# Attention with chunk selection, then a gated MLP, on one core: K^T of two head pairs made on TensorE instead of by DMA, under a new instruction order

## The chip, the cores and the metric

The kernel runs on one core of one Trainium2 chip. The metric is the device time of one launch in microseconds. The core has TensorE (PE; its weight loads are PEld), VectorE (DVE), ScalarE (ACT), GpSimd (POOL) and SyncE (SP), which here issues all DMAs. Matmul results land in PSUM, everything else lies in SBUF.

## What is computed

q, k and v are 4 x 8 x 768 x 64 (batch, heads, positions, head width), in float32. Keys are taken in 24 chunks of 32. For every query an upper bound of its score with each chunk is taken from the chunk's minimum and maximum of k; the six best chunks are kept, the rest is masked, and a causal softmax attention runs over what is left. Its output goes through a gated block with a spatial mix.

```python
ub = sum(maximum(q * k_min, q * k_max))          # per query and chunk
top_chunks = argsort(where(causal, ub, -1e9))[..., -6:]
attn = softmax(where(selected & causal, q @ k.T / 8, -1e9))
x = attn @ v                                     # 4 x 768 x 512
h = gelu(x @ w_in); u, v = h[..., :512], h[..., 512:]
v_n = (v - mean(v)) / sqrt(var(v) + 1e-6) * g_ln
out = x + (u * (w_sg @ v_n + b_sg)) @ w_out
```

## The kernel before, in words

**Pairs and batches.** The 32 heads are worked on in 16 pairs p of two heads; pairs 4b to 4b + 3 make batch b. Position blocks are 128 long (six of them). For each pair the program has K^T and Q^T in bf16 (tiles KA and QA, four buffers, index p % 4), V with a column of ones (vx), the selection, six score pieces (PSUM tiles PSC, two buffers), exponentials into E (ScalarE, L784 and L833), a triangle set to zero on the diagonal blocks (POOL, L789 and L840), P V (TensorE, L856 and L863), and a division into XS (VectorE, L871 and L873; below "rcp" and "xs"). When the four pairs of a batch are done, x is transposed (TensorE L890 for batches 0 and 3, DMA L882 for 1 and 2; "dt_x") and the MLP runs: hv (L905, the half that is normalised), hu (L945), the mix pt (L962) with two VectorE steps (L968, L972), the output ou (L981), the residual sum os (L988) and the store (L992).

**Two ways to K^T.** For pairs below KD = 8, `kside` loads k in two DMAs, transposes it on TensorE in float32 (L524, "ktr"), takes each chunk's minimum and maximum from PSUM on VectorE (L563, "kmm"), and copies K^T out of PSUM to KA ("kev": four copies of 64 x 384 for pairs 4 and up). From pair KD on, `kside_full` loads k in one DMA, takes minimum and maximum with a transposing reduction (L580, "kred"), casts k to bf16 with mask columns beside it (tile kbx, or the tile of IND used again; "kcast"), and lets SP issue two DMA transposes into KA (L587, "kT"). The reductions of two pairs are then put in place by one group of small matmuls (L602, "perm") and two copies (L610, "wcp"). Both ways end in W, with a small subtraction ("wsub", L573 or L615).

**Selection.** From pair 4 on, two pairs are selected together (`select_full`): the bounds by small matmuls (L709, "ub"), a transpose (L718, "utr"), the eight largest (L729, "m8"), a comparison (L734, "dn"), a transpose back (L737, "dt"), and four small DMAs that write the mask rows into QA (L742, "qd"; qd_8_1 is pair 8, head 1). The scores of the pair ("sc", L778) wait for them.

**Order.** Nothing is scheduled at run time. The table TABLE holds, for each of the five engines, the numbers of its operations in the order in which they run, a PSUM slot for each tile, and, under "engine", the engine of those copies and casts that could run on more than one (`flex`, L435 to L438: a name such as kev_4_0_0 or qcast_3 with act or dve; without an entry the copy has its usual engine). `Program.place` takes order and slots, `Program.link` works out the semaphore waits. Engines that touch the same PSUM tile wait for each other in program order, also when both only read. On each engine, and in SP's queue, everything behind a waiting instruction waits too.

Of the kernel before, what the change touches and what calls it, by code (L numbers as in the profile page):

```python
# [261 lines left out]
def _build(nc, ctx, q, k, v, w_in, g_ln, w_sg, b_sg, w_out, out):  # L262
# [46 lines left out]
    NBULK = 0  # L309
    XROW = 940  # L310
    DXT = tuple((b, d) for b in (1, 2) for d in range(4))
    KD = 8
    WSGT = False
    GROUPS = [(0,), (1,), (2,), (3,)] + [(a, a + 1) for a in range(4, NP, 2)]
    NW = 4
# [430 lines left out]
    def mask_rows(w):  # L746

        for i in range(2):
            m0 = 64 * (1 - i)
            if w + HALF < KD:  # L750
                flex("pool", ("act",), lambda i=i, m0=m0: KA[w][i][m0:m0 + 64, :], lambda m0=m0: INDF[m0:m0 + 64, :], S,
# [268 lines left out]

    if KD < NP:
        kb_init(0)
# [24 lines left out]
    for p in range(4, NP + 4):  # L1047
# [19 lines left out]

TABLE = {
# [16 lines left out]
    "act": (  # L1085
# [10 lines left out]
    "dve": (  # L1096
# [16 lines left out]
    "pool": (  # L1113
# [13 lines left out]
    "slots": (  # L1127
        "10230231221303100111101110030212010101231013110010132121001110101032100101010103200010112322333223233223"
        "22322333232201110033100011112311100101100123001100012310011023233232232233323233333233220100102201111000"
        "23101010110101231010110032100101232332322223332332332323232210101023000110122000110123101011123020301213"  # L1130
        "33210130111302021102"),
    "filler": (
        "49:8 "),
    "engine": (
        "rel_0:act rel_1:act wic_0:act kcast_9_0:act rel_7:act rel_6:act woc_0:act kcast_8_0:act qcast_7_1:act "
        "qcast_6_0:act kcast_9_1:act rel_8:act kcast_8_1:act kcast_11_0:act qcast_10_0:act rel_11:act "
        "vhat_1_2:act vhat_1_0:act kcast_13_1:act qcast_12_0:act rel_14:act vcast_14:act vhat_3_3:act "
        "vhat_3_5:act vhat_3_0:act qev_0_1:dve kev_0_1:dve kev_2_1:dve qev_2_1:dve wev_1_1:dve qev_2_0:dve "
        "wev_1_0:dve qev_4_0:dve kev_4_1_0:dve kev_4_0_0:dve xev_0_0:dve wev_0_0:dve qev_5_1:dve kev_5_0_0:dve "
        "kev_5_0_1:dve kev_5_1_1:dve vhat_0_3:dve vhat_0_4:dve vhat_0_1:dve vhat_0_0:dve vhat_0_2:dve "  # L1140
        "qev_10_1:dve qev_13_0:dve xev_3_0:dve xev_3_2:dve "),
}


# [57 lines left out]
```

## Time and profile before

| | us |
|---|---|
| median of 3 runs | 223.46 |
| their lowest and highest | 222.56, 226.68 |
| the profiled execution | 224.85 |
| its span, first to last instruction | 223.1 |

In the views of the profile "busy" is the time in which an engine's instructions ran; "idle before" is the time in which it stood before an instruction, with what ended that wait; "x" counts instructions. L778 is line 778. A name out<-in tells the tile that is written and those that are read. SPq is SP's queue of DMA issues. The span is also cut into 40 equal slices of 5.6 us, and a digit tells the busy share of each in tenths.

### The profile page before, as it was taken

The numbers are of one execution on the slowest core, as the hardware profiler recorded it, in microseconds if no ns is written. First come the engines' busy times: TensorE is split into PE (matmuls) and PEld (weight loads), VectorE is DVE, ScalarE is ACT, GpSimd is POOL, SyncE is SP. The second block draws the span as 40 slices with busy tenths as digits, with TensorE's granted clock in tenths as the row PEclk, the third lists the DMA queues.
The fourth block names the chain that finished last, engine by engine and source line by source line (L and its number), as shares of the span: only waits on it lengthen the run. The fifth ranks groups of instructions, "written<-read, shape, count | busy, mean of one in ns | idle before, by whom it ended". The sixth has DMA issues, their size and how long they took to land.

```text
span 223.1 us, 6031 instructions
## 1 busy us (share of the span) xinstructions
PE 203.6 (91%) x2397; PEld 131.1 (59%) x2397; DVE 185.3 (83%) x526; ACT 165.3 (74%) x247; POOL 96.4 (43%) x135
## 2 busy tenths in 40 slices
PE   7689959989999999885999999999799999999993
PEld 3456738855765657664445676776544668655551
DVE  4999972979999999899599998875699776695993
ACT  3879857997899997895768986986966888667000
POOL 7626877595224367476113076745233124002000
PEclk9999996999999999999699999999999999999999
DMA  7999999979269999799999969938941103000306
GB/s 153 218 250 209 268 208 325 347 164 207 87 159 242 239 233 217 169 175 150 201 201 180 254 135 226 228 92 207 162 101 28 36 0 144 3 0 0 144 29 253
DMA packets 101403, 37.06 MB, mean 166 GB/s; under 512 B 95616, under 2 KB 96384, under 8 KB 101376
## 3 DMA queue, kind: packets, MB, share of 16 engines
q1 hardware_dynamic: 101376, 36.68, 76.7%
q8 instruction: 19, 0.31, 0.6%
q14 instruction: 8, 0.07, 0.1%
HBM read 24.77 MB, written 6.29 MB: 139 GB/s over the span
## 4 chain that ended last, share of the span: by engine, by line
PE 62%; DVE 20%; DMA 6%; ACT 5%; SPq 3%; issue 2%; POOL 1%; DVEq 0%
PE PSG L962 12%; PE PSG L905 9%; PE PSC L778 8%; PE PSG L981 6%; PE PSG L945 5%; PE PSG L524 5%; PE PSG L856 4%; DVE Wall L563 3%; PE PSC L818 3%; ACT E L784 2%; DMA out_dram<-osb 2%; PE PSG L709 2%; DMA kn<-in_k_dram 2%; DVE U L718 2%; DVE osb L988 2%
## 5 line engine op out<-in xcount | busy, mean ns | idle before, releaser
L784 ACT ACTIVATE E<-PSC 128x1024 bf16<-128x1024 f32 (+1 forms) x72 | 62.8, 919 | 13.4 <-PE PSC L778 10.8
L778 PE MATMUL PSC<-QA,KA 128*128 128x128 bf16 (+2 forms) x336 | 37.4, 247 | 3.6 <-DMA QA<-Dt 2.1
L789 POOL TENSOR_SCALAR_AFFINE_SELECT E<-E 128x768 bf16<-128x768 bf16 x24 | 21.0, 879 | 37.4 <-ACT E L784 37.4
L962 PE MATMUL PSG<-wsgT,vhat 128*128 128x384 bf16 x192 | 34.8, 326 | 0.5 <-DVE rden L871 0.5
L778 PEld LDWEIGHTS PSC<-QA,KA 128*128 128x128 bf16 x336 | 23.8, 98 | 14.4 <-ACT E L784 5.1
L438 POOL CAST QA<-qT 64x768 bf16<-64x768 f32 (+1 forms) x24 | 21.2, 885 | 13.9 <-DVE qT L438 4.9
L962 PEld LDWEIGHTS PSG<-wsgT,vhat 128*128 128x128 bf16 x192 | 18.0, 98 | 11.2 <-ACT uT L950 0.6
L905 PE MATMUL PSG<-winb,xT 128*128 128x512 bf16 x96 | 23.0, 384 | 1.8 <-issue 1.3
L945 PE MATMUL PSG<-xT,winb 128*128 128x384 bf16 x128 | 23.7, 327 | 0.0
L950 ACT ACTIVATE uT<-PSG 128x384 bf16<-128x384 f32 x32 | 15.2, 487 | 11.2 <-PE PSG L945 11.0
L981 PE MATMUL PSG<-woutb,uT 128*128 128x512 bf16 x96 | 23.4, 379 | 0.1
L968 DVE SCALAR_TENSOR_TENSOR PSG<-PSG,glnT,bsgbc 128x384 f32<-128x384 f32 x32 | 19.7, 618 | 4.1 <-PE PSG L962 3.5
L833 ACT ACTIVATE E<-PSC 128x1024 bf16<-128x1024 f32 (+1 forms) x24 | 20.7, 924 | 3.0 <-PE PSC L824 2.9
L856 PE MATMUL PSG<-vx,E 128*128 128x65 bf16 x480 | 20.2, 195 | 1.6 <-DVE XS L873 1.3
L988 DVE TENSOR_TENSOR osb<-PSG,XS 128x512 f32<-128x512 f32 x24 | 16.0, 684 | 6.4 <-PE PSG L981 4.7
L856 PEld LDWEIGHTS PSG<-vx,E 128*128 128x128 bf16 x480 | 17.9, 99 | 3.7 <-DVE XS L873 1.8
L909 ACT ACTIVATE vgb<-PSG 128x512 f32<-128x512 f32 x24 | 14.0, 597 | 7.5 <-PE PSG L905 7.4
L563 DVE TENSOR_REDUCE Wall<-PSG 128x12 f32<-128x384 f32 x32 | 16.0, 543 | 2.7 <-PE PSG L524 2.6
L873 DVE TENSOR_TENSOR XS<-PSG,rden 128x384 bf16<-128x384 f32 x32 | 17.6, 552 | 0.7
L972 DVE TENSOR_TENSOR uT<-PSG,uT 128x384 bf16<-128x384 f32 x32 | 17.4, 551 | 0.5
L945 PEld LDWEIGHTS PSG<-xT,winb 128*128 128x128 bf16 x128 | 11.5, 98 | 9.4 <-ACT uT L950 2.1
L524 PE MATMUL PSG<-identF,qn 128*128 128x128 f32 x96 | 15.1, 278 | 1.7 <-DMA qn<-in_q_dram 1.0
(107 smaller groups left out, 363.1 us busy)
## 6 DMA issues: line engine op xcount, KB each, us to landing
qn<-in_q_dram SPq DMA_DIRECT2D x32, 192.0 KB, 4.1
vn<-in_v_dram SPq DMA_DIRECT2D x16, 384.0 KB, 5.2
out_dram<-osb SPq DMA_DIRECT2D x24, 256.0 KB, 2.3
kn<-in_k_dram SPq DMA_DIRECT2D x16, 192.0 KB, 4.6
kn<-in_k_dram SPq DMA_DIRECT2D x8, 384.0 KB, 4.1
uT<-in_moe_w_sg_dram SPq DMA_DIRECT2D x4, 384.0 KB, 6.5
vgb<-in_moe_w_in_dram SPq DMA_DIRECT2D x3, 512.0 KB, 6.2
QA<-Dt SPq DMA_DIRECT2D x24, 36.0 KB, 2.7
```

The costliest lines, as they stand in the source:

```text
L438: return e.tensor_copy(dst(), src())
L524: r = e.matmul(t.ap()[:, 128 * j:128 * j + 128], src[:].rearrange("p i t d -> p (i t d)")[:, 128 * x:128 * x + 128], identF[:], is_transpo ...
L563: P.op("dve", lambda d, m=m, op=op, t=t, hf=hf: d.tensor_reduce(W[w][:, m, 12 * hf:12 * hf + 12], t.ap()[:, 0:TG].rearrange("p (c x) -> p ...
L778: r = e.matmul(t.ap()[:, o:o + n], KA[w][i][:, 128 * kb:128 * kb + 128], QA[w][i][:, q0:q0 + n], start=True, stop=True)
L784: P.op("act", lambda e, t=t, c0=c0, c1=c1, i=i: e.activation(E[es][:, i, c0:c1], t.ap()[:, 0:c1 - c0], ACTF.Exp, scale=SCALE), act(c1 - c0 ...
L789: P.op("pool", lambda g, ev=ev: g.affine_select(ev, ev, pattern=[[0, NT], [1, 128]], compare_op=ALU.is_ge, fill=0.0, base=0, channel_multi ...
L833: P.op("act", lambda e, t=t, c0=c0, c1=c1, n=n: e.activation(E[es][:, :, c0:c1], t.ap().rearrange("p (i x) -> p i x", i=2)[:, :, 0:n], ACT ...
L856: r = e.matmul(t.ap()[:, 65 * qb:65 * qb + 65], E[es][:, i, a:a + 128], vx[w][:, kb, i, :], start=first, stop=False, skip_group_check=True)
L905: r = e.matmul(t.ap()[:, 0:F], xT[s][:, dk, 128 * qt:128 * qt + 128], winb[:, dk, F:DFF], start=(dk == 0), stop=(dk == NDK - 1))
L945: r = e.matmul(t.ap()[:, 0:TG], winb[:, dk, 128 * fb:128 * fb + 128], xT[s][:, dk, TG * tg:TG * tg + TG], start=(dk == 0), stop=(dk == NDK ...
L962: r = e.matmul(t.ap()[:, 0:TG], vhat[s][:, sb, 128 * fb:128 * fb + 128], wsgT[:, sb, TG * tg:TG * tg + TG], start=(sb == 0), stop=(sb == N ...
L981: r = e.matmul(t.ap()[:, 0:DM], gT[s][:, fb, 128 * qt:128 * qt + 128], woutb[:, fb, :], start=(fb == 0), stop=(fb == NF - 1))
```

## The change

KD goes from 8 to 10, so pairs 8 and 9 get their K^T in the first of the two ways. This renumbers the operations, and the whole table is replaced: the order on every engine, the PSUM slots, and the list of engines. No operation is computed otherwise than before apart from pairs 8 and 9.

```diff
-    KD = 8
+    KD = 10
...
     "engine": (
-        "rel_0:act rel_1:act wic_0:act kcast_9_0:act rel_7:act rel_6:act woc_0:act kcast_8_0:act qcast_7_1:act "
-        "qcast_6_0:act kcast_9_1:act rel_8:act kcast_8_1:act kcast_11_0:act qcast_10_0:act rel_11:act "
-        "vhat_1_2:act vhat_1_0:act kcast_13_1:act qcast_12_0:act rel_14:act vcast_14:act vhat_3_3:act "
-        "vhat_3_5:act vhat_3_0:act qev_0_1:dve kev_0_1:dve kev_2_1:dve qev_2_1:dve wev_1_1:dve qev_2_0:dve "
-        "wev_1_0:dve qev_4_0:dve kev_4_1_0:dve kev_4_0_0:dve xev_0_0:dve wev_0_0:dve qev_5_1:dve kev_5_0_0:dve "
-        "kev_5_0_1:dve kev_5_1_1:dve vhat_0_3:dve vhat_0_4:dve vhat_0_1:dve vhat_0_0:dve vhat_0_2:dve "
-        "qev_10_1:dve qev_13_0:dve xev_3_0:dve xev_3_2:dve "),
+        "qcast_0:act mrow_0_1_0:act rel_1:act qcast_3:act wic_0:act rel_5:act mrow_3_0_0:act qcast_4_0:act "
+        "rel_6:act rel_7:act kcast_10_1:act woc_2:act woc_3:act rel_8:act rel_10:act rel_11:act qcast_11_0:act "
+        "rel_12:act vhat_1_0:act kcast_13_1:act rel_13:act kcast_13_0:act rel_14:act vhat_3_2:act vhat_3_5:act "
+        "kev_0_0:dve qev_0_0:dve kev_2_1:dve kev_2_0:dve qev_2_0:dve kev_3_1:dve kev_4_0_1:dve kev_4_0_0:dve "
+        "kev_4_1_0:dve kev_4_1_1:dve kev_5_0_1:dve xev_0_0:dve qev_5_1:dve kev_5_0_0:dve xev_0_1:dve xev_0_3:dve "
+        "kev_5_1_1:dve kev_5_1_0:dve kev_7_1_0:dve vhat_0_3:dve vhat_0_5:dve vhat_0_4:dve vhat_0_1:dve "
+        "vhat_0_0:dve qev_15_0:dve xev_3_0:dve xev_3_1:dve xev_3_2:dve xev_3_3:dve "),
```

The rest of the table are numbers. In names, and to the point of the prediction, the orders read as follows (before, then after; each engine by itself, excerpts).

```
PE    ub_8 sc_7_1_2 ... pv_7_1 pvd_7_1 pv_7_0 pvd_7_0 qtr_12_1 qtr_12_0 sc_8_1_0 sc_8_1_1 ub_10 sc_8_1_2 hv_1_1
PE    perm_10 ... ub_8 ... pv_7_0 pvd_7_0 pv_7_1 pvd_7_1 qtr_12_1 qtr_12_0 ub_10 sc_8_1_2 sc_8_1_0 hv_1_1

DVE   utr_8 m8_8_0 m8_8_1 rcp_6_1 dn_8 xs_6_1 rcp_6_0 dt_8 xs_6_0 rcp_7_1 xs_7_1 rcp_7_0 xs_7_0
DVE   utr_8 m8_8_1 rcp_6_0 m8_8_0 xs_6_0 rcp_6_1 xs_6_1 dn_8 dt_8 rcp_7_0 xs_7_0 rcp_7_1 xs_7_1

POOL  kcast_11_1 qcast_9_0 aff_6_0 aff_7_1 qcast_8_0 kcast_10_1 aff_7_0
POOL  aff_6_0 vcast_6 kcast_11_0 vcast_8 aff_7_0 aff_6_1 vcast_7 aff_7_1 qcast_10_1

SP    kT_8_1 qn_12_1 kT_8_0 kn_14 dt_x_1_1 dt_x_1_0 qd_8_1 dt_x_1_2 dt_x_1_3 qn_13_0 qd_8_0
SP    dt_x_1_0 qn_13_0 qn_12_1 vn_7 qn_11_1 dt_x_1_1 kn_12 dt_x_1_2 qd_8_1 dt_x_1_3 qn_13_1 qd_8_0

SP    qn_1_0 kn_2_0 kn_2_1 qn_2_1 qn_3_0 qn_2_0 qn_3_1 ws_1
SP    qn_1_1 ws_1 kn_2_1 kn_2_0 qn_3_1 qn_2_1 qn_2_0 qn_3_0
```

(kn, qn and vn load a pair's k, q and v; qtr transposes q on TensorE; aff is the triangle of E; ws loads a tile of w_sg; vcast and qcast cast v and q to bf16.)

More of the change, by code (lines that the diff above doesn't have):

```diff
@@ L1069 @@
     "pe": (
[15 rows of a table removed]
-    "act": (
[10 rows of a table removed]
-    "dve": (
[16 rows of a table removed]
-    "pool": (
[13 rows of a table removed]
[15 rows of a table added]
+    "act": (
[10 rows of a table added]
+    "dve": (
[17 rows of a table added]
+    "pool": (
[12 rows of a table added]
     "slots": (
[L1128 to L1131, printed above, removed]
+        "23102213010323200101101110130011110010232110001110123120310010010032011111010102300110103332323232322232"
+        "33223222332301100032000000111023111101011010320110011032101010232332332233222333333222323210011033100111"
+        "10321001010111012311101000320101012323323332232223322233232233001110231001101321110010320100101231213003"
+        "2032111012311302030302"),
     "filler": (
```

106 rows, old and new, of the table TABLE are left out of this document.

## The prediction

> **What bounds the kernel now.** I read the page first (busy shares, the 40 slices), then the busy time by stage, then the chain of waits and the timeline at the two places where TensorE stops, then the groups by line and shape for prices.
>
> ```profile
> span 223.1 us, 6031 instructions
> PE 203.6 (91%) x2397; PEld 131.1 (59%) x2397; DVE 185.3 (83%) x526; ACT 165.3 (74%) x247; POOL 96.4 (43%) x135
> PE   7689959989999999885999999999799999999993
> PEclk9999996999999999999699999999999999999999
> ```
>
> TensorE is busy 91% of the span: 19.5 us are left. Its digits fall at the start, in slices 6 and 19 (a 5 each) and in the last one, and the granted clock has a 6 in the slice behind each of the two 5s. The stretches below (columns: window and its length, then busy us of PE, PEld, DVE, ACT, POOL, clock, DMA share, GB/s) are my stages: up to the last transpose of x for batch 0, up to the selection of pairs 8 and 9, up to the MoE of batch 1, up to the MoE of batch 2, and the rest.
>
> ```profile
> 0.00:46.60 46.60, 39.36 (x605) 28.23 (x605) 36.49 (x120) 35.59 (x52) 31.14 (x52) 0.96 1.05 241
> 46.60:93.65 47.05, 45.02 (x490) 29.49 (x490) 44.48 (x128) 41.54 (x72) 23.04 (x33) 1.00 0.88 196
> 93.65:109.00 15.35, 11.73 (x204) 7.99 (x203) 12.32 (x39) 11.35 (x16) 8.93 (x12) 0.91 1.02 162
> 109.00:159.70 50.70, 48.53 (x621) 31.22 (x620) 43.35 (x134) 42.03 (x59) 21.41 (x27) 0.99 1.01 188
> 159.70:223.10 63.40, 58.98 (x482) 34.17 (x482) 48.61 (x108) 34.80 (x51) 11.93 (x13) 0.99 0.24 73
> ```
>
> The second stage is full on two engines (TensorE 45.0 and VectorE 44.5 of 47.05), so work added there counts in full. The fourth and fifth are TensorE's, with 2.2 us idle and, in the fifth, 3.7 us of stores behind the last matmul. Time can be won in the first and the third. What happens there:
>
> ```profile
> 31.45 0.54 DVE L438 CAST KA<-PSG 64x384 bf16<-64x384 f32 x1
> 32.02 0.48 ACT L435 ACTIVATE KA<-PSG 64x384 bf16<-64x384 f32 x1 [2.53 <-DVE KA L438]
> 32.52 1.30 ACT L833 ACTIVATE E<-PSC 128x1024 bf16<-128x1024 f32 x2
> 33.60 0.39 PE L818 MATMUL PSC<-QA,KA 64*128 64x384 bf16 x4 [2.64 <-ACT E L833]
> ```
>
> ScalarE stood 2.53 us before one copy of pair 4's K^T, because VectorE held the same PSUM tile for its half of it; the exponentials queue behind that copy on ScalarE, and the scores of pair 2 (TensorE, 2.64 us idle) wait for an exponential to free their PSUM. In the third stage:
>
> ```profile
> 98.08 1.99 DVE Dn L734
> 100.69 1.29 SPq L882
> 102.03 3.34 DMA QA<-Dt
> 105.42 1.05 PE PSC L778 x11
> 106.47 2.10 PE PSG L709 x32
> ```
>
> This is the chain of pair 8: compare (Dn), transpose, the small DMA that puts the mask rows into QA (it stood in SP's queue behind an x transpose), then the scores. Both stops are followed by a slow clock:
>
> ```profile
> 31.00:33.60 2.60, 0.00 (x1) 0.01 (x2) 1.37 (x4) 1.57 (x3) 2.37 (x4) 1.00 0.76 168
> 33.60:38.60 5.00, 5.00 (x73) 4.21 (x73) 1.43 (x5) 3.78 (x7) 4.00 (x5) 0.66 1.08 322
> 105.42:109.10 3.68, 3.68 (x47) 1.83 (x48) 1.03 (x2) 1.94 (x2) 0.00 (x0) 0.63 0.73 160
> 155.00:160.00 5.00, 3.73 (x82) 2.71 (x64) 3.26 (x16) 4.98 (x7) 0.05 (x1) 1.00 1.00 131
> ```
>
> At 0.66 for 5.00 us and 0.63 for 3.68 us the lost clock is 5.00 x 0.34 = 1.7 us and 3.68 x 0.37 = 1.4 us. The stop of 1.27 us before 159.7 (last row: 5.00 - 3.73) is followed by none.
>
> **The change, part by part.** *K^T of pairs 8 and 9.*
>
> ```profile
> L580 DVE TRANSPOSE_TENSOR_REDUCE Bn<-kn 128x24 f32<-128x768 f32 x16 | 15.2, 962 | 0.0
> L563 DVE TENSOR_REDUCE Wall<-PSG 128x12 f32<-128x384 f32 x32 | 16.0, 543 | 2.7 <-PE PSG L524 2.6
> L610 DVE COPY Wall<-PSG 128x48 f32<-128x48 f32 x8 | 1.4, 201 | 0.7 <-PE PSG L602 0.7
> L524 PE MATMUL PSG<-identF,kn 128*128 128x128 f32 x48 | 7.5, 282 | 1.6 <-DMA kn<-in_k_dram 1.0 <-ACT KA L435 0.6
> L602 PE MATMUL PSG<-Bn,identF 64*32 64x24 f32 x128 | 1.6, 191 | 0.0
> L435 ACT ACTIVATE KA<-PSG 64x384 bf16<-64x384 f32 x11 | 5.3, 481 | 2.7 <-DVE KA L438 2.5
> L435 ACT ACTIVATE kbx<-kn 128x384 bf16<-128x384 f32 x2 | 1.1, 542 | 0.0
> L587 SPq DMA_TRANSPOSE KA<-kbx x8: 1248/1290/2101, 93.8 to 159.9; - x8
> L742 SPq DMA_DIRECT2D QA<-Dt x24: 507/591/2139, 59.7 to 173.3; - x24
> ```
>
> TensorE: 12 transposes come, 12/48 x 7.5 = 1.9 us; one group of 32 small matmuls goes, 32/128 x 1.6 = 0.4: +1.5 us, in the full second stage: on the path. VectorE: 8 reductions come, 8/32 x 16.0 = 4.0; 4 long ones go, 4/16 x 15.2 = 3.8; two 201 ns copies go and one small subtraction comes: about even, 0. ScalarE: 8 copies come, 8 x 0.481 = 3.8; 4 casts go, 4 x 0.542 = 2.2: +1.7 us, beside TensorE (41.5 of 47.05 busy); if that cover were gone it would cost all of it. SP's queue: 4 transposes at 1.29 us go, and two whole loads of K are split into four. Nobody waits for these transposes (pair 8's scores wait for QA<-Dt), so I cost the freed queue at nothing; the ends are 0 and 4 x 1.29 = 5.2 us of earlier issues.
>
> *Other engines.* Over the whole kernel VectorE is handed 18 movable copies and gives 15; ScalarE takes five casts of 768 columns from POOL ahead of its first gelu (qcast_0, qcast_3, qcast_4_0, two mask rows) and gives two 768-column evictions of x; the rest goes one for one.
>
> ```profile
> L435 ACT ACTIVATE QA<-qT 64x768 bf16<-64x768 f32 x4 | 3.3, 836 | 0.0
> L435 ACT ACTIVATE xT<-PSG 128x768 bf16<-128x768 bf16 x5 | 4.0, 809 | 2.1 <-PE PSG L890 2.1
> L438 DVE CAST KA<-PSG 64x384 bf16<-64x384 f32 x5 | 2.7, 546 | 0.0
> ```
>
> ScalarE in the first stage: 35.6 + 5 x 0.84 - 2 x 0.81 = 38.2 us. VectorE there is handed ten and gives eight, 36.5 + 2 x 0.55 = 37.6 us.
>
> *First stage in the new order.* All four quarter-copies of pair 4's K^T now lie on VectorE, so ScalarE no longer stands before one of them, and the exponentials run on. The gain is at most the stop and its clock, 2.6 + 1.7 = 4.3 us. TensorE's work there is the same, 39.4 - 1.7 = 37.7 us at full clock, with VectorE 37.6 and ScalarE 38.2: three engines equally full trip over each other, and w_sg's second tile is now loaded ahead of pair 2's K. What is late next is VectorE's K^T and q copies of pairs 4 and 5. I take -2.5 us, nearer to the full price, since the copy that caused it is gone; ends -4.3 and +2.6 (ScalarE's extra work with its 11.0 us of idle time kept).
>
> *Second stage.* +1.5 us, as above; ends 0 (its 2.0 us of idle time take it) and +3.
>
> *Third stage.* The selection matmuls of pairs 10 and 11 (L709, the 2.10 us row, 1.2 us at full clock) now stand ahead of pair 8's scores instead of behind, and so fill the stop; xs_6 goes ahead of dn_8 on VectorE, so that pair 7's P V no longer waits for it:
>
> ```profile
> 100.60 0.64 PE L856 MATMUL PSG<-vx,E 128*128 128x65 bf16 x15 [0.91 <-DVE XS L873]
> 101.80 0.62 PE L856 MATMUL PSG<-vx,E 128*128 128x65 bf16 x15 [0.38 <-DVE XS L873]
> 105.42 1.05 PE L778 MATMUL PSC<-QA,KA 128*128 128x128 bf16 x11 [2.13 <-DMA QA<-Dt]
> ```
>
> But the chain grows by one xs (0.55 us), and qd_8_1 now stands behind three x transposes in SP's queue, of which the last is ready before dn_8. Idle is 0.91 + 0.38 + 2.13 = 3.4 us plus 1.4 of clock. Filling 1.2 of it is sure if the chain keeps its length; the shorter stop may spare the clock. I take -1.5; ends -4.8 (all of it) and +2.1 (rival 3).
>
> The page "TensorE: Matmul & The Clock Gate" of the Trainium skill, Part 1, says that the clock falls after an idle window of about 3.4 us that runs free. Here stops of 2.64 and 2.13 us were enough and 1.27 was not, so the measurement decides; if the page's figure were a threshold, no stop here would pay for a slow clock, and the sum would be about 1 us less of a gain.
>
> *Fourth and fifth stage.* Same instructions in nearly the same places on TensorE; the stop before batch 2's MoE waits for x transposes that hang on pair 11's heads, as before. 0; ends -1 and +3, since an order this dense can get a new wait of the size of the two above.
>
> **The sum.** -2.5 + 1.5 - 1.5 + 0 = -2.5 us. The profiled execution took 224.85 us (span 223.1 and 1.75 around it), so one like it would take 222.4; the median of the runs shown is 223.46, 1.4 below, so I forecast 221.0.
>
> **The rivals.** (1) *Both stops go in full*, the second with its clock (2.13 + 1.4 = 3.5): -4.3 + 1.5 - 3.5 = -6.3, 217.2 us. For it: both have one named cause, which the order takes away. Against: three engines within 0.6 us of each other in the first stage. (2) *ScalarE becomes the bound of the first stage* and that stage gets longer: its waits for TensorE and VectorE stay at 46.6 - 35.6 = 11.0 us and its work grows by 2.6: +2.6 + 1.5 - 1.5 = +2.6, 226.1 us: slower than before. It decides once ScalarE's idle time up to the first gelu stays above 46.6 - 38.2 = 8.4 us. For it: five casts from an idle POOL to a busier engine. Against: 2.53 us of that idle time had the cause that goes. (3) *dn_8 is held by POOL.*
>
> ```profile
> L734 DVE TENSOR_TENSOR Dn<-U,m x6: 740/758/2053, 55.4 to 162.5; 128x576 bf16<-128x576 f32 x6
> 97.78 1.68 POOL L789 TENSOR_SCALAR_AFFINE_SELECT E<-E 128x768 bf16<-128x768 bf16 x2
> ```
>
> dn_8 took 2.05 us where the other five took about 0.76, and POOL ran two selects back to back over its start. So it lost 1.3 us. In the new order POOL has four such instructions in a row there, 4 x 0.84 = 3.4 us: the chain of pair 8 can grow by 3.4 - 1.3 = 2.1: -2.5 + 1.5 + 2.1 = +1.1, 224.6 us. It decides if dn_8 comes up while all four are still to run; against it, dn_8 now stands behind two more instructions of VectorE. "SBUF — State Buffer" of the Trainium skill, "SBUF: two separate sides", has the rule: VectorE with two SBUF inputs and GpSimd take one shared port pair in turn, for a whole instruction; the 2.05 us agree.
>
> **How the numbers follow.** Chances: forecast 0.45 (218.5 to 223.5), rival 1 0.20, rival 2 0.20, rival 3 0.15. The range takes in part of each end: 216.0 to 227.5 us. 2% is 4.5 us, about what a measurement of this kernel can tell from no change. Below 219.0: most of rival 1 and a little of the forecast, 0.20; above 227.9: the upper ends of rivals 2 and 3, 0.14; within, 0.66.
>
> **What would show it.** In the profile after: no stop of over 1 us on L818 near 30 us and no 6 in PEclk's slice 7; the x transposes of batch 0 end before 45 us; the second stage is some 1.5 us longer at the same fullness; the scores of pair 8 follow L709 with a stop below 1.5 us. The prediction is wrong if ScalarE idles over 8.4 us before its first gelu, if Dn of pair 8 takes over 2 us again with a longer stop behind it, or if L524 waits for the loads of K longer than the 1.0 us of its row above.

## The result and the profile after

| | before | after |
|---|---|---|
| median of 20 runs each, us | 224.47 | 220.87 |
| lowest and highest, us | 222.43, 226.68 | 219.73, 223.8 |
| the profiled execution, us | 224.85 | 220.88 |
| its span, us | 223.1 | 218.8 |

The ratio is 0.985, with a 95% interval of 0.982 to 0.988: 1.5% faster, about 3.3 us. The forecast was 221.0 us. The profiled execution of the kernel before lay 0.4 us above its median, so the two profiles differ by 0.4 us more than the medians.

The page of the kernel after, its busy shares and its slices:

```profile
span 218.8 us, 5980 instructions
PE 199.7 (91%) x2363; PEld 131.0 (60%) x2377; DVE 187.1 (85%) x532; ACT 166.6 (76%) x251; POOL 93.5 (43%) x132
PE   7599999989999997987996999998898999999992
PEclk9999999999999999999999999999999999999999
```

Both 6s in PEclk are gone, and TensorE's busy time fell from 203.6 to 199.7 us although it has more to do: it no longer runs at a slow clock. I now cut the span at the same five events in every kernel: the first bound matmul (L709) of pair 4, that of pair 8, the first matmul of the MLP (L905) of batch 1, that of batch 2, the end. Busy time by these stages, first of the kernel before, then of the kernel after (columns as in the prediction: window, length, busy PE, PEld, DVE, ACT, POOL, clock):

```profile
0.00:48.86 48.86, 40.94 (x612) 28.85 (x612) 38.69 (x125) 37.83 (x55) 33.15 (x55) 0.97 1.04 238
48.86:93.65 44.79, 43.44 (x483) 28.87 (x483) 42.29 (x123) 39.30 (x69) 21.03 (x30) 1.00 0.89 197
93.65:108.91 15.26, 11.64 (x204) 7.89 (x203) 12.23 (x39) 11.35 (x16) 8.93 (x12) 0.92 1.02 162
```

```profile
0.00:45.60 45.60, 39.68 (x611) 27.33 (x612) 39.95 (x126) 39.37 (x58) 28.31 (x50) 1.00 1.11 250
45.60:91.65 46.05, 44.18 (x463) 30.03 (x466) 43.74 (x124) 42.38 (x74) 24.89 (x35) 1.00 0.87 199
91.65:103.81 12.16, 10.11 (x198) 7.45 (x196) 10.97 (x40) 9.43 (x15) 6.34 (x8) 1.00 1.02 151
103.81:154.91 51.10, 47.25 (x617) 31.90 (x623) 42.67 (x137) 42.12 (x60) 25.01 (x31) 1.00 0.95 170
154.91:218.80 63.89, 58.49 (x477) 34.29 (x482) 49.78 (x109) 33.30 (x49) 8.95 (x9) 1.00 0.28 81
```

The first stage is 3.3 us shorter, the second 1.3 longer, the third 3.1 shorter; the fourth and fifth (50.74 and 63.45 us before) are 0.4 longer each. The sum is -4.3 us of span. What became of the first stop (timeline of the kernel after; columns: start, length, engine, line, operation, and in brackets the idle time before it):

```profile
28.73 1.12 DVE L438 CAST KA<-PSG 64x384 bf16<-64x384 f32 x2
29.17 0.39 PE L818 MATMUL PSC<-QA,KA 64*128 64x384 bf16 x4
...
31.29 1.94 ACT L833 ACTIVATE E<-PSC 128x1024 bf16<-128x1024 f32 x2
32.84 0.39 PE L818 MATMUL PSC<-QA,KA 64*128 64x384 bf16 x4
```

VectorE makes the copies of pair 4's K^T, ScalarE goes from exponential to exponential, and no score stands idle. The last x transpose of batch 0 ends at 43.3 us, where it was 46.6. The second stage has a new stop, the third none above 0.8 us on the rows of L709, L778 and L905 (the same view):

```profile
82.33 0.39 SPq L511 DMA_DIRECT2D kn<-in_k_dram  x1
83.16 0.53 SPq L742 DMA_DIRECT2D QA<-Dt  x1
87.59 1.84 DVE L580 TRANSPOSE_TENSOR_REDUCE Bn<-kn 128x24 f32<-128x768 f32 x2 [0.75 <-DMA kn<-in_k_dram]
87.82 0.45 PE L778 MATMUL PSC<-QA,KA 128*128 128x256 bf16 x3 [1.33 <-DMA QA<-Dt]
...
97.12 0.75 DVE L734 TENSOR_TENSOR Dn<-U,m 128x576 bf16<-128x576 f32 x1
98.71 0.54 SPq L742 DMA_DIRECT2D QA<-Dt  x1
...
101.53 0.72 PE L709 MATMUL PSG<-qT,Wall 64*32 64x288 f32 x16 [0.73 <-ACT qT L435]
102.67 0.89 PE L778 MATMUL PSC<-QA,KA 128*128 128x256 bf16 x10
104.04 1.24 PE L905 MATMUL PSG<-winb,xT 128*128 128x512 bf16 x5 [0.47 <-DMA xT<-XS]
```

The load of pair 11's k (82.33) waits for pair 8's transposes, qd_6_1 stands behind it in SP's queue, and the scores of pair 6 wait 1.33 us for qd_6_1. In the third stage the bounds of pairs 10 and 11 go ahead of pair 8's scores, as forecast, and Dn takes 0.75 us.

### The profile page after: what moved, and what is told of

Its sections match the earlier page's. It is cut to its first block, busy times and chain, and to the rows that moved or that the text cites. A ratio compares the mean times of both kernels' runs of the same rounds, so it can differ in the third digit from the quotient of the medians.

```text
span 218.8 us, 5980 instructions
## 1 busy us (share of the span) xinstructions
PE 199.7 (91%) x2363; PEld 131.0 (60%) x2377; DVE 187.1 (85%) x532; ACT 166.6 (76%) x251; POOL 93.5 (43%) x132
## 4 chain that ended last, share of the span: by engine, by line
PE 55%; DVE 25%; DMA 9%; issue 3%; POOL 3%; SPq 2%; ACT 2%; DVEq 0%
PE PSG L962 15%; PE PSC L778 9%; PE PSG L981 8%; PE PSG L524 5%; PE PSG L856 4%; DVE vhat L933 4%; DVE Wall L563 3%; DVE stats L914 3%; DMA kn<-in_k_dram 3%; PE PSG L905 3%; PE PSG L945 2%; PE PSG L709 2%; DMA QA<-Dt 2%; DMA out_dram<-osb 2%; PE PSG L863 2%
## 5 line engine op out<-in xcount | busy, mean ns | idle before, releaser
L778 PE MATMUL PSC<-QA,KA 128*128 128x128 bf16 (+2 forms) x336 | 36.5, 246 | 1.7 <-DMA QA<-Dt 1.3
L778 PEld LDWEIGHTS PSC<-QA,KA 128*128 128x128 bf16 x336 | 24.0, 98 | 11.5 <-ACT E L784 2.4
L945 PE MATMUL PSG<-xT,winb 128*128 128x384 bf16 x128 | 24.2, 327 | 0.0
L438 POOL CAST QA<-qT 64x768 bf16<-64x768 f32 (+1 forms) x24 | 20.6, 862 | 8.2 <-PE PSC L778 4.0
L905 PE MATMUL PSG<-winb,xT 128*128 128x512 bf16 x90 | 21.4, 379 | 2.0 <-issue 0.8
L563 DVE TENSOR_REDUCE Wall<-PSG 128x12 f32<-128x384 f32 x40 | 20.6, 542 | 2.9 <-PE PSG L524 2.8
L981 PE MATMUL PSG<-woutb,uT 128*128 128x512 bf16 x88 | 21.8, 379 | 0.4
L856 PE MATMUL PSG<-vx,E 128*128 128x65 bf16 x480 | 19.7, 194 | 0.9 <-DVE osb L988 0.9
L920 POOL TENSOR_TENSOR rstd<-rstd,neghalf 128x6 f32<-128x6 f32 x4 | 5.3, 1329 | 31.9 <-DVE rstd L918 31.9
L438 POOL CAST vx<-vn 128x768 bf16<-128x768 f32 x16 | 14.0, 879 | 8.2 <-DMA vn<-in_v_dram 8.0
```

The costliest lines, as they stand in the source:

```text
L438: return e.tensor_copy(dst(), src())
L563: P.op("dve", lambda d, m=m, op=op, t=t, hf=hf: d.tensor_reduce(W[w][:, m, 12 * hf:12 * hf + 12], t.ap()[:, 0:TG].rearrange("p (c x) -> p ...
L778: r = e.matmul(t.ap()[:, o:o + n], KA[w][i][:, 128 * kb:128 * kb + 128], QA[w][i][:, q0:q0 + n], start=True, stop=True)
L856: r = e.matmul(t.ap()[:, 65 * qb:65 * qb + 65], E[es][:, i, a:a + 128], vx[w][:, kb, i, :], start=first, stop=False, skip_group_check=True)
L905: r = e.matmul(t.ap()[:, 0:F], xT[s][:, dk, 128 * qt:128 * qt + 128], winb[:, dk, F:DFF], start=(dk == 0), stop=(dk == NDK - 1))
L945: r = e.matmul(t.ap()[:, 0:TG], winb[:, dk, 128 * fb:128 * fb + 128], xT[s][:, dk, TG * tg:TG * tg + TG], start=(dk == 0), stop=(dk == NDK ...
```

## The experiments

In the diffs the numbers of the order table are written as names of operations. "Before" beside a run is the kernel before, run on the same chip at the same time; the ratio to it is what kernels are compared by (the kernel after: 0.985). Two profiled executions of the same instructions differ: the first stage of the kernels made from the changed one, where nothing was edited, took 45.3 to 46.0 us, and that of the runs with the copy moved and with both moves, which is the same in the two, took 46.09 and 44.73 us. A single stage is therefore read to about 0.5 us at best, and the first was once 1.4 us off.

**One copy on another engine.** KD stays 8.

```diff
-ACT   ... exp_2_1 kev_4_0_1 exp_2_0 exp_2_5 ...
+ACT   ... exp_2_1 exp_2_0 exp_2_5 ...
-DVE   ... kev_4_0_0 dt_3 ...
+DVE   ... kev_4_0_0 kev_4_0_1 dt_3 ...
```

> The kernel before with one copy moved: kev_4_0_1 from ScalarE to VectorE, right behind kev_4_0_0. Theory (order): the 2.64 us stop before L818 near 31 us shrinks below 1 us, and no slow clock follows; the time falls by 2 to 4 us against the kernel before. Rival (K^T): the gain of the changed kernel comes from the four DMA transposes and their casts that went; then this run gains nothing (0 +- 0.7 us). Third possibility: another wait takes the place of the stop, with a gain of 0.5 to 1.5 us and a stop of over 1 us elsewhere before 40 us.

220.84 us against 223.84, ratio 0.985 (0.981 to 0.990). Its PEclk, scores and ScalarE at the place:

```profile
PEclk9999999999999999999999999999999999999999
30.04 1.30 ACT L833 ACTIVATE E<-PSC 128x1024 bf16<-128x1024 f32 x2 [0.17 <-PE PSC L824]
31.27 0.39 PE L818 MATMUL PSC<-QA,KA 64*128 64x384 bf16 x4
```

The stop and the slow clock behind it are gone, and one moved instruction gains as much as the whole change. The theory of the first stage holds; the rival, that the gain comes from K^T, does not.

**The bounds ahead of the scores.** Alone on the kernel before, and together with the moved copy.

```diff
-PE    ... qtr_12_0 sc_8_1_0 sc_8_1_1 ub_10 sc_8_1_2 hv_1_1
+PE    ... qtr_12_0 ub_10 sc_8_1_0 sc_8_1_1 sc_8_1_2 hv_1_1
```

> The kernel before with one operation moved on TensorE: ub_10 ahead of sc_8_1_0. Theory (order): ub_10 fills 1.2 us of the 2.13 us stop before pair 8's scores and what is left no longer lowers the clock; the time falls by 1.2 to 2.6 us. Rival (the stop is set by the chain of pair 8 and what is behind it): hv_1_1 starts no earlier, since the scores free their PSUM at the same time as before, and the time falls by less than 0.5 us.

225.0 us against 223.84, ratio 1.007 (1.003 to 1.011): no gain, and a small loss. Its timeline:

```profile
104.60 0.72 PE L709 MATMUL PSG<-qT,Wall 64*32 64x288 f32 x16 [0.82 <-ACT qT L435]
106.05 1.05 PE L778 MATMUL PSC<-QA,KA 128*128 128x128 bf16 x11 [0.25 <-DMA QA<-Dt]
107.56 0.59 SPq L501 DMA_DIRECT2D qn<-in_q_dram  x1
111.87 0.52 PE L524 MATMUL PSG<-identF,qn 128*128 128x128 f32 x3 [1.20 <-issue]
```

The stop is filled as planned and the clock stays up, so hv_1_1 starts 0.9 us earlier; but the q transpose of pair 13, whose load is issued at 107.56 behind four x transposes, starts at 111.87 us where it was 111.8 before. All of it is given back there. The rival was right about the size, for another reason than it gave.

> Both moves of the two runs beside it, KD still 8. Theory (order): the two gains add up, -3.5 to -6 us against the kernel before, so as fast as the changed kernel or up to 2 us faster than it, since the dearer K^T of pairs 8 and 9 is not paid. Rival (K^T): no gain, 0 +- 0.7 us.

221.44 against 223.84, ratio 0.989 (0.984 to 0.994): the first move's gain, and nothing from the second.

**KD = 10 alone.** The order and the engines of before, with the new operations put in by hand.

```diff
-    KD = 8
+    KD = 10
-PE    ... ou_0_0 sc_5_0_0 ... sc_5_1_2 pv_4_0 pvd_4_0 pv_5_0 ...
+PE    ... ou_0_0 ktr_8_0 ktr_8_1 sc_5_0_0 ... sc_5_1_2 ktr_9_0 pv_4_0 pvd_4_0 ktr_9_1 pv_5_0 ...
-DVE   ... m8_6_1 os_0_1 os_0_0 m8_6_0 os_0_2 ... os_0_5 kred_10_0 ...
+DVE   ... m8_6_1 kmm_8_0_0 kmm_8_0_1 os_0_1 os_0_0 m8_6_0 kmm_8_1_0 kmm_8_1_1 wsub_8 os_0_2 ... os_0_5 kmm_9 (4) wsub_9 kred_10_0 ...
-ACT   ... qcast_6_0 kcast_9_1 rel_8 kcast_8_1 qev_10_0 ... exp_5_1_2 ...
+ACT   ... qcast_6_0 kev_8_0 (2) rel_8 kev_8_1 (2) qev_10_0 ... exp_5_1_2 kev_9 (4) ...
```

> KD = 10 alone: the kernel before with pairs 8 and 9 made the first way, their transposes and copies placed by hand at 80 to 91 us, all other operations in the order and on the engines of before. Theory (order): slower by 0.5 to 3 us, nearest 1.5 (12 more float32 transposes at 0.16 us in a full stage, and VectorE's 8 reductions now late in that stage instead of 4 early ones). Rival (K^T): faster by 2 to 4 us.

231.38 against 223.84, ratio 1.032 (1.026 to 1.038): 7.5 us slower, where 0.5 to 3 were expected. Its second and third stage, and the longest stop:

```profile
49.51:102.17 52.66, 47.26 (x461) 31.45 (x464) 44.39 (x126) 41.53 (x73) 20.39 (x29) 0.94 0.78 168
102.17:115.13 12.96, 10.45 (x204) 7.69 (x203) 12.47 (x42) 12.55 (x18) 9.79 (x13) 1.00 0.64 102
```

```profile
86.57 1.54 PE L524 MATMUL PSG<-identF,qn 128*128 128x128 f32 x6 [2.15 <-ACT KA L435]
```

My places were bad: the reductions stand ahead of pair 6's selection on VectorE, the copies keep PSUM from the q transposes, and the second stage grows by 7.9 us. That says nothing about a good order. But the third stage is 2.3 us shorter (12.96 for 15.26), in the old order and without any of the moves that I had counted on there. That can't be put to the freed queue alone. About 1.2 us of the 15.26 are the slow clock (15.26 x 0.08), which this run does not have there (1.00); and behind a second stage that is so much longer the DMA engines have less to do (share 0.64 for 1.02).

**The four DMA transposes put back.** In the changed kernel, four transposes of a constant tile into free space go into SP's queue, first ahead of pair 11's second q load, then (second diff) behind it.

```diff
-SP    ... qd_7_1 qn_11_0 dt_x_1_0 qn_13_0 qn_12_1 vn_7 qn_11_1 dt_x_1_1 ...
+SP    ... qd_7_1 qn_11_0 xk_0 dt_x_1_0 qn_13_0 xk_1 qn_12_1 xk_2 vn_7 qn_11_1 xk_3 dt_x_1_1 ...
```

```diff
+SP    ... qd_7_1 qn_11_0 qn_11_1 xk_0 dt_x_1_0 qn_13_0 xk_1 qn_12_1 xk_2 vn_7 xk_3 dt_x_1_1 ...
```

> The changed kernel with four DMA transposes put back into SP's queue between 87 and 93 us, about where those of pairs 8 and 9 stood before; they copy a constant tile into free space, and nobody reads them. Theory of the prediction (the freed queue is worth nothing): within 0.4 us of the changed kernel. Rival (the freed queue is part of the third stage's gain, since x transposes and q loads come up behind them): slower by 1 to 3 us, with hv_1_1 later by as much and a longer stop at qd_8 or at the q transposes.

225.98 against 224.67, ratio 1.010 (1.006 to 1.014): slower than the changed kernel by 2.5% (1.010 / 0.985), 5 to 6 us, and so by more than the 1 to 3 us of the rival. The q load, issued 5.8 us later than there, and its transpose:

```profile
96.68 1.00 SPq L502 DMA_DIRECT2D qn<-in_q_dram  x1
...
101.25 0.52 PE L525 MATMUL PSG<-identF,qn 128*128 128x128 f32 x3 [3.91 <-issue]
```

> As the run with the four transposes put back, but with the load that then came late (qn_11_1) moved ahead of all four, so that they stand in front of loads and x transposes that have some slack. Theory of a slack queue (only the one late load made the loss of 5 us): within 0.5 us of the changed kernel, 220.5 to 221.5. Rival (the queue has no 5 us to give at this place, whatever is ahead): 1.5 to 4 us slower than the changed kernel, with qd_8_1 or the last x transposes later by as much.

224.92 against 225.81, ratio 1.000 (0.996 to 1.004): still 1.5% slower than the changed kernel. Its third stage, and where it stops:

```profile
91.61:106.23 14.62, 11.03 (x198) 8.26 (x195) 11.25 (x40) 9.02 (x14) 6.29 (x8) 0.88 1.01 171
```

```profile
94.74 0.99 SPq L512 DMA_DIRECT2D vn<-in_v_dram  x1
100.53 0.61 PE L857 MATMUL PSG<-vx,E 128*128 128x65 bf16 x15 [2.68 <-POOL vx L439]
101.89 0.59 SPq L743 DMA_DIRECT2D QA<-Dt  x1
```

Now v of pair 7 is late (issued at 94.74 for 90.32 in the changed kernel), qd_8_1 is issued at 101.89 for 98.71, and a stop of 2.68 us lowers the clock to a mean of 0.88. The third stage lasts 14.62 us for 12.16: most of the gain of that stage is gone, with all orders as in the changed kernel but for these DMAs and the one load. The stops cost part of this through the clock: its mean is 0.90 and 0.88 over the two stages, about 1.7 us of each (16.86 x 0.10, 14.62 x 0.12). The clock is not the whole loss; the two executions of the second kernel with a mean clock of 1.0 took 224.1 us, 3 us more than the changed kernel's median. The third stage in all kernels:

| kernels | third stage, us |
|---|---|
| KD 8: before; copy moved; bounds moved; both; both and other queue order (below) | 15.26; 14.43; 14.54; 14.82; 13.45 |
| KD 10: by hand; after; the five variants of after below | 12.96; 12.16; 11.50 to 12.51 |
| after, four transposes back: two places | 16.86; 14.62 |

**SP's queue in another order, KD 8.** On top of both moves.

```diff
-SP    ... kT_8_1 qn_12_1 kT_8_0 kn_14 dt_x_1_1 dt_x_1_0 qd_8_1 dt_x_1_2 dt_x_1_3 qn_13_0 qd_8_0 qn_13_1 kn_13 ...
+SP    ... kT_8_1 qn_12_1 qn_13_1 qn_13_0 dt_x_1_1 dt_x_1_0 qd_8_1 dt_x_1_2 dt_x_1_3 kT_8_0 qd_8_0 kn_14 kn_13 ...
-POOL  ... kcast_11_1 qcast_9_0 aff_6_0 aff_7_1 qcast_8_0 kcast_10_1 aff_7_0 qcast_11_0 kcast_10_0 qcast_11_1
+POOL  ... aff_6_0 qcast_9_0 aff_7_1 qcast_8_0 kcast_11_1 kcast_10_1 aff_7_0 qcast_11_0 qcast_11_1 kcast_10_0
-DVE   ... kred_12_1 kred_14_0 kred_12_0 ... dn_10 dt_10 ...
+DVE   ... kred_12_1 kred_12_0 ... dn_10 dt_10 kred_14_0 ...
```

> The kernel of the run with both moves (KD 8), with what then held its third stage moved aside: in SP's queue the loads of q for pair 13 go ahead of the four x transposes, kT_8_0 and kn_14 behind them; on POOL aff_6_0 goes ahead of two casts that wait for a DMA; kred_14_0 goes behind dt_10 on VectorE. Theory (the third stage is set by SP's queue: x transposes stood 1.5 us behind their data there and qtr_13_1 waited 1 us for its load): faster than that run by 1 to 2.5 us, 219 to 220.5 us where the kernel before takes 223.8. Rival (it is set by the chain of pair 8 and pair 7's P V): no faster than that run, 221.0 to 221.9.

222.6 against 224.67, ratio 0.992 (0.989 to 0.996): not faster than the run with both moves. The third stage is 1.4 us shorter than there (13.45 for 14.82), and the fourth 2.3 longer (54.42 for 52.08): what was pushed back in the queue is waited for later:

```profile
114.61 0.40 PE L602 MATMUL PSG<-Bn,identF 64*32 64x24 f32 x32 [0.77 <-DVE Bn L580]
116.53 0.55 PE L524 MATMUL PSG<-identF,qn 128*128 128x128 f32 x3 [0.77 <-DVE Wall L610]
```

**The price of K^T on TensorE.** The transposes of pairs 8 and 9 twice; and two thirds of their work left out.

```diff
-                P.op("pe", rows_T(kn[s], t, hf, KRUN[p]), pe32(*[128] * 3), ("ktr", p, hf), ...
+                P.op("pe", twice(rows_T(kn[s], t, hf, KRUN[p])) if p >= 8 else rows_T(kn[s], t, hf, KRUN[p]), ...
```

> The changed kernel, with the four groups of float32 transposes of pairs 8 and 9 issued twice, so with 12 transposes more between 77 and 84 us. Theory (the second stage is full on TensorE, so added work there counts in full): slower than the changed kernel by 1.2 to 1.9 us (4 groups of 0.31 us, or 12 times 0.16). Rival (they hide in stops that this stage has anyway, such as the 1.6 us one at 87 us): slower by less than 0.5 us.

221.81 against 224.67, ratio 0.989 (0.984 to 0.994), 0.35% or 0.8 us above the changed kernel, with intervals that overlap. Its second stage:

```profile
45.99:93.03 47.04, 45.36 (x478) 31.47 (x478) 44.15 (x124) 42.76 (x75) 24.77 (x35) 1.00 0.91 197
```

Twelve more transposes make TensorE 45.36 - 44.18 = 1.2 us busier, 0.10 us each, and the stage 1.0 us longer. The third stage is 0.7 us shorter (11.50 for 12.16), little more than two executions differ by. The 0.8 us lie between the two theories (1.2 to 1.9, and under 0.5), so the run decides for neither.

```diff
+        n = 1 if p in (8, 9) else 3
-            for j in range(3):
+            for j in range(n):
-                        W[w][:, m, 12 * hf:12 * hf + 12], t.ap()[:, 0:TG] ...
+                        W[w][:, m, 12 * hf:12 * hf + 4 * n], t.ap()[:, 0:128 * n] ...
```

> The changed kernel with two thirds of the K^T work of pairs 8 and 9 left out (one of three transposes, reductions and copies of 128 of 384 columns each; so K^T and chunk bounds of these pairs are not what the reference needs). It keeps every instruction's place and wait. Theory (the added work counts in full in the second stage): ub_8 comes 1 to 2 us earlier than in the changed kernel, and the time falls by about as much, 219 to 220. Rival (the added work costs by what waits behind it, not by its length): ub_8 less than 0.5 us earlier, no change of time.

220.32 against 225.81, ratio 0.980 (0.974 to 0.985): 0.6% below the changed kernel, again within the intervals. Its stop at the known place:

```profile
87.51 0.45 PE L779 MATMUL PSC<-QA,KA 128*128 128x256 bf16 x3 [1.73 <-DMA QA<-Dt]
```

The second stage is only 0.3 us shorter than in the changed kernel (45.73 for 46.05), since the stop behind qd_6_1 grows from 1.33 to 1.73 us. Of the two theories the second fits that stage: work saved ahead of a DMA is waited for at the DMA.

**The new stop of the second stage.**

```diff
-SP    ... kn_13 qd_6_0 st_0_0 st_0_1 kn_11 qd_6_1 qn_12_0 ...
+SP    ... kn_13 qd_6_0 qd_6_1 st_0_0 st_0_1 kn_11 qn_12_0 ...
```

> The changed kernel with one DMA moved in SP's queue: qd_6_1 right behind qd_6_0, ahead of two stores and of kn_11, which waits there for ktr_8_1. Theory (the 1.3 to 1.6 us stop before sc_6_1_2 at 87.8 us is the price of qd_6_1 standing behind kn_11): that stop goes and the time falls by 0.7 to 1.5 us against the changed kernel. Rival (kred_11, which waits for kn_11, and the selection behind it are late anyway): the stop goes and comes back before ub_8; less than 0.4 us.

222.18 against 224.67, ratio 0.993 (0.989 to 0.997): 0.8% slower than the changed kernel. The stop before the scores is gone, and comes back two microseconds later:

```profile
87.95 1.84 DVE L580 TRANSPOSE_TENSOR_REDUCE Bn<-kn 128x24 f32<-128x768 f32 x2 [0.99 <-DMA kn<-in_k_dram]
89.84 0.40 PE L602 MATMUL PSG<-Bn,identF 64*32 64x24 f32 x32 [1.01 <-DVE Bn L580]
```

As the rival had it, pair 11's k is late anyway: its load takes 5.0 us to land, and the reductions and the small matmuls wait for it.

**The longest stop of the fourth stage**, 1.89 us before the mix at 119 us.

```diff
-DVE   ... kred_14_0 kred_15_0 nmr_1 vhat (5) kred_14_1 kred_15_1 vs_1_0_1 gt_1_0_1 vs_1_1_0 gt_1_1_0 ...
+DVE   ... kred_14_0 nmr_1 vhat (5) kred_14_1 vs_1_0_1 gt_1_0_1 kred_15_0 vs_1_1_0 gt_1_1_0 kred_15_1 ...
-PE    ... pt_1_1_0 perm_14 sc_8_0_0 pt_1_0_2 sc_8_0_2 pt_1_1_2 ...
+PE    ... pt_1_1_0 sc_8_0_0 pt_1_0_2 sc_8_0_2 pt_1_1_2 perm_14 ...
```

> The changed kernel with the longest stop of its fourth stage taken away: at 119 us the mix (L962) waits 1.9 us for vhat, and on VectorE nmr and the five vhat stand behind kred_15_0, which waits 1.1 us for its load. Here kred_15_0 and kred_15_1 go behind the first two gates, and perm_14 behind the third mix. Theory (the stop is set by that wait): pt_1_0_1 starts 1.0 to 1.4 us earlier and the time falls by 0.8 to 1.4 us, to 219.5 to 220.1. Rival (what follows, ub_12 or batch 2's MoE, hangs on something else): pt_1_0_1 earlier, hv_2_0 not; less than 0.4 us.

222.63 against 225.81, ratio 0.989 (0.985 to 0.993): no gain. The stop shrinks to 0.54 us, and the q transpose of pair 15 stops instead; its load stands behind two small DMAs that wait for pair 10's selection, and lands about when the transpose starts (the row names VectorE, which was done at 131.70):

```profile
119.50 2.11 PE L962 MATMUL PSG<-wsgT,vhat 128*128 128x384 bf16 x12 [0.54 <-DVE vhat L933]
126.76 0.58 SPq L501 DMA_DIRECT2D qn<-in_q_dram  x1
131.91 0.52 PE L524 MATMUL PSG<-identF,qn 128*128 128x128 f32 x3 [0.87 <-DVE PSG L968]
```

**All named loads first.**

```diff
-SP    ... kn_13 qd_6_0 st_0_0 st_0_1 kn_11 qd_6_1 ... qn_11_0 dt_x_1_0 qn_13_0 qn_12_1 vn_7 qn_11_1 ... qn_15_1 vn_12 qd_10_0 qd_11_0 qn_15_0 ...
+SP    ... kn_13 qd_6_0 qd_6_1 st_0_0 st_0_1 kn_11 ... qn_11_0 qn_11_1 dt_x_1_0 qn_13_0 qn_12_1 vn_7 ... qn_15_1 qn_15_0 vn_12 qd_10_0 qd_11_0 ...
-PE    ... ktr_9_0 pv_4_1 ktr_8_1 ...
+PE    ... ktr_8_1 pv_4_1 ktr_9_0 ...
-DVE   ... kred_14_0 kred_15_0 nmr_1 vhat (5) kred_14_1 kred_15_1 ...
+DVE   ... kred_14_0 nmr_1 vhat (5) kred_14_1 kred_15_0 kred_15_1 ...
```

> The changed kernel with the waits moved that the runs so far named: in SP's queue qd_6_1 right behind qd_6_0, qn_11_1 behind qn_11_0, qn_15_0 behind qn_15_1; ktr_8_1 and its reductions and copies change places with ktr_9_0 and its own, so that kn_11's load starts earlier; kred_15_0 behind kred_14_1, so that vhat no longer waits for a load. Theory (TensorE's stops left in the changed kernel are loads that stand too far back in SP's queue, and the gain of one is given back at the next): with all four moved, ub_8 comes 0.7 to 1.3 us earlier, pt_1_1_0 1.2 to 2 us, and the time falls by 1 to 2 us, to 0.976 to 0.981 of the kernel before. Rival (what is won up to there is given back before batch 2's MoE, whose x transposes hang on pair 11's heads): hv_2_0 less than 0.4 us earlier and no faster than the changed kernel, 0.985.

221.95 against 225.42, ratio 0.987 (0.980 to 0.993): as fast as the changed kernel, not faster. kn_11 was issued no earlier (83.15 us), its reduction waited 1.33 us, and at batch 2's MLP the stop was 1.96 us where the changed kernel has 0.84 (at 155.15):

```profile
88.49 1.84 DVE L580 TRANSPOSE_TENSOR_REDUCE Bn<-kn 128x24 f32<-128x768 f32 x2 [1.33 <-DMA kn<-in_k_dram]
156.41 0.81 PE L905 MATMUL PSG<-winb,xT 128*128 128x512 bf16 x3 [1.96 <-issue]
```

The theory that the remaining stops are loads too far back, and worth a microsecond or two, fails as a plan; the rival is right.

## Why the prediction was right, and where not

**The time** was right: 221.0 forecast, 220.87 measured, and "within 2%" was the likeliest class. That the two agree to 0.1 us is luck. The forecast started from 223.46 us, the median of three runs, and took off 2.5; the kernel before measured 224.47 beside the changed one, which took off 3.6 (3.3 by the ratio). A start 1.0 us too low and a gain 1.1 us too small cancel. The steps, read from the two profiles, were off one by one: -3.3 for -2.5, +1.3 for +1.5, -3.1 for -1.5, +0.8 for 0, together -4.3 us of span.

**First stage, -2.5 forecast, -3.3 in the profiles.** Right in mechanism: the signs named beforehand are there (no stop over 1 us on L818, no 6 in slice 7, the x transposes before 45 us), and the run with one copy moved shows the cause by itself. The size was cut down for fear that three full engines would trip over each other. They did not: TensorE, VectorE and ScalarE were busy for 39.7, 40.0 and 39.4 of 45.6 us. Rival 2 (ScalarE becomes the bound) needed over 8.4 us of idle time on ScalarE; it had 45.6 - 39.4 = 6.2. Rival 1 (both stops go in full) came near in both stages, -3.3 for its -4.3 and -3.1 for its -3.5. Its 217.2 us did not come: of the 2.0 us that the span lacks, the first stage has 1.0, the third 0.4 and the later ones 0.8, and the second gives 0.2.

**Second stage, +1.5 forecast, +1.3 measured.** The size was right, the working only in part. A transpose costs 0.10 us there and not the 0.16 that I took from the mean of all 48, so TensorE's work is not 1.5 but 44.18 - 43.44 = 0.7 us more. The rest is idle time: 1.87 us where it was 1.35, with the 1.33 us stop behind kn_11 and qd_6_1 as its largest piece. I had given the doubt about the loads of K one clause at the end, and no price.

**Third stage, -1.5 forecast, -3.1 measured. The step that failed is this one: "Nobody waits for these transposes (pair 8's scores wait for QA<-Dt), so I cost the freed queue at nothing".** Nobody waits for the four transposes, but q loads, v loads, qd_8_1 and x transposes stand behind them in the same queue. Put back into the new order, they lengthen the stage by 2.5 and 4.7 us, where my range for the free queue had gone from 0 to 5.2 us and the sum had taken 0. What the runs show is that the new order has no room for them. What they cost in the order before is not shown: there SP's queue stood waiting as well (2.2 us for VectorE ahead of the second x transpose), and KD 8 with the queue in another order, the four transposes still in it, brought the stage to 13.45 us. How much of the 3.1 us is the free queue and how much the new order stays open.

The reason that I did give, the bounds ahead of the scores, gains nothing by itself (ratio 1.007). About 1.2 us of the 3.1 are the clock, 0.92 before (15.26 x 0.08) and 1.00 after; the run with only the copy moved has no slow clock either, and its stage took 14.43 us. I also misread the orders: ahead of dn_8 the changed kernel has two more xs and one rcp, not one xs. These, and the new order on POOL, were not tried alone. Rival 3 did not come: Dn took 0.75 us.

**Fourth and fifth stage, 0 forecast, +0.8 measured**, within the ends of -1 and +3. The cause is not settled; two profiles differ by as much.

**Where the gain comes from.** One copy moved on the kernel before takes the same time as the whole change, ratio 0.985 each. Against that run, the changed kernel's second stage is 2.2 us longer (46.05 for 43.90) and its third 2.3 shorter (12.16 for 14.43). So the gain of the whole change has the size of what one copy gives, taken off an engine that had to wait for it, and KD = 10 with the rest of the order comes to about nothing. That K^T's price in the second stage is paid back by the freed queue in the third is my reading of two single profiles whose orders differ throughout; it is argued, not shown. Whether KD = 10 could win in another order, or KD = 8 with the full planned order, was not tried.

The slow clock is not where the gain lies either. The two stretches at half clock in the profile of before are not in all of its executions: in 9 of the 81 that ran beside the experiments the mean clock was 0.996 or more, and their median is 223.97 us, 0.7 below that of all 81. The 13 executions of the changed kernel with such a clock have a median of 220.4 us. The difference, about 3.5 us, is that of the medians.

## What to carry to other kernels

Before pricing a large change, look for the one instruction in an in-order engine that waits for another engine with work queued behind it: here it was worth 3 us of 224, as much as a new order of everything. A queue has a price even when nobody waits for the entry that goes: ask what stands behind it. And where every stage is nine tenths full, look at the next load before filling a stop: of the five runs here that moved what a later stop waited for (the bounds, SP's queue in another order, qd_6_1 first, vhat first, all loads first), none was faster than the kernel it was made from, and in each a stop stood at a later place.

## What the runs showed of the hardware

From 20 us on, the clock fell after every stop of TensorE of 2.1 us or more: 2.64 and 2.13 in the kernel before, 2.89 with the bounds moved, 2.49 and 2.15 with KD = 10 by hand, 3.91 and 2.68 in the runs with four transposes back. In no profiled execution did it fall there after a stop of up to 1.97 us. How it fell is plainest around the 2.15 us stop of KD = 10 by hand, cut where the clock changes (window, length, busy PE, PEld, DVE, ACT, POOL, clock):

```profile
82.26:85.67 3.41, 1.21 (x7) 0.31 (x4) 3.38 (x17) 1.79 (x4) 0.00 (x0) 1.00 0.69 201
85.67:89.08 3.41, 2.51 (x14) 2.21 (x15) 2.09 (x4) 1.41 (x4) 0.00 (x0) 0.50 0.60 148
89.08:92.50 3.42, 3.42 (x11) 1.65 (x10) 1.20 (x2) 2.24 (x3) 2.41 (x4) 0.50 0.56 126
92.50:95.91 3.41, 3.36 (x54) 2.79 (x54) 2.63 (x5) 1.27 (x3) 2.06 (x4) 1.00 0.00 0
95.91:99.33 3.42, 1.70 (x34) 1.35 (x31) 3.35 (x8) 3.37 (x6) 0.41 (x1) 1.00 0.58 130
```

The clock is at half speed for whole stretches of 3.41 us, here for two. The first follows a stretch in which TensorE was busy for 1.21 us; it has 2.51 us of work itself, and a second slow one follows; behind a full one the clock is up again. A stretch with 1.70 us of work (95.91) was not followed by a slow one. In the kernel before, the stretches ahead of the two falls have 1.09 and 1.28 us of work (31.28 to 34.69, 102.96 to 106.37), and in the changed kernel that with the 1.89 us stop has 1.52 (116.77 to 120.18) and no fall. So whether a stop of about 2 us costs another 1.7 us (3.41 x 0.5, an estimate) hangs on how it lies in these stretches, and not on its length alone. The rule is not complete: before 20 us, four profiled executions have a slow stretch with no stop over 1.4 us ahead of it (qd_6_1 first: 9.34 to 12.76, behind 1.77 us of work). "TensorE: Matmul & The Clock Gate" of the Trainium skill, Part 1, has half speed until TensorE has been busy for a window of about 3.4 us, and these rows agree. It has the fall after an idle window of the same length; there the runs differ, since a window with 1.21 us of work in it was enough.

The small DMA of the mask rows takes 2.3 us to land in the median of the kernel after, and a k load of 384 KB 5.2 (list of its DMAs: count, size, median us to landing):

```profile
QA<-Dt SPq DMA_DIRECT2D x24, 36.0 KB, 2.3
kn<-in_k_dram SPq DMA_DIRECT2D x6, 384.0 KB, 5.2
```

Issued right behind such a load (83.16 behind 82.33) the mask rows of pair 6 were awaited until 87.8 us, 4.6 us later, about when the load landed (82.33 + 5.2 = 87.5). And Dn of pair 8 took 0.75 us in the changed kernel, where no POOL instruction ran beside it, and 2.05 before, beside two selects. That agrees with the rule on the shared port in "SBUF — State Buffer" of the Trainium skill, "SBUF: two separate sides".
